# Decayed attention into a snake layer: first state in a bank of its own, 64x64 state products, diagonal states in six more blocks, and a new order

## The chip, the core and the metric

One core of a Trainium2 chip. The metric is the device time of one execution in microseconds (us). Before the change three runs gave 211.56 us in the median (211.51 to 212.55).

## What is computed

Attention with a decay `lam` per head, without softmax, over 4 batches, 8 heads, 768 positions and 64 columns, block by block with a running state, and behind it one layer of a network whose activation is h + sin(alpha h)^2 / alpha. All inputs are float32.

```python
for b in range(nb):
    intra = einsum(einsum(qb, kb) * Dmask, vb)
    inter = (qb * lam_pow) @ kv_state
    out[:, :, sl] = intra + inter
    kv_state = lam_block * kv_state + (kb * rev_pow).T @ vb
x = out as (3072 tokens, 512)
h = x @ w_in                       # 512 -> 2048
g = h + sin(alpha * h) ** 2 / alpha
result = g @ w_out                 # 2048 -> 512
```

## The kernel before

**Attention.** The kernel works with blocks of 128 positions, six to a batch, 24 in all (numbers s = 0 to 23; n = s % 6 is the place in the batch). The decay is folded into q and k when they are scaled (scale_block, L454), so that the state is a plain sum. For each block there are four kinds of work:

- S, the scores (part_S, L601): PE multiplies k by q for 8 heads into two PSUM banks, and DVE multiplies the result by a mask into the tile Sm (L623).
- O, the output (part_O, L678): PE adds v times Sm (L716) and the state times q, and ACT or DVE copies the sum from its bank into xT (L726), the input of the layer.
- Z, the state (part_Z, L637): PE adds k times v into bank 7 (ZB = 7, L1061). The bank keeps the running sum through a batch; after each block the state so far is copied out for the next block's O.
- transposes of q and k, on PE for blocks below 12 (piece_Q, piece_K, piece_T) and by DMA (L501) from block 12 on.

A state can be copied out in two forms. `diag(s)` (L630) chooses: the diagonal form goes in two halves (L666) into the tile Zd, [128, 4, 128], in which two heads stand on the diagonal of a 128x128 square and zeros beside them; O then needs four full products (`inter`, L692, matmul at L694), which `run` (L574) issues ahead of everything else in the group. The compact form is one copy (L672) into Zc, and O then needs eight products on 64x64 corners of the array (L707), behind the scores. With SD = 12 the blocks 0 to 5 and 12 to 23 are diagonal, and 6 to 11 compact.

The products of Z differ as well. Blocks 0 to 5 take four products of 128 columns, two heads by two heads, of which only the diagonal squares are used (L648; blocks 0 to 3, whose q, k and v lie two positions to a partition, take them twice with 64 rows each). Blocks from 6 on take eight products of 64 columns, one for each head (L656).

Blocks 0 to 3 are worked at the start, before the layer, from L1073 on: scores (piece_S, L790), states (piece_Z, L793), v times Sm for two blocks at once (piece_P, L746, matmul at L759), then the state's part (piece_I, L772, matmul at L779), and the copies into xT (evict, L734, copy at L739). State 0 goes into bank 7, is copied, state 1 is added in the same bank, is copied, and so on. From block 4 on, piece_G (L800) joins S of one block with O and Z of the block before.

**The layer.** Tokens go in six chunks of 512. unit_A (L807, matmul at L822) and unit_A2 (L845, matmul at L856; two output rows of half a chunk) make one or two of 16 rows of h in a bank; ACT takes the sine (L832, L866), ACT or POOL its square (L836, L837, L870, L871), and DVE adds it to h in the bank, into gT (L839, L874), which frees the bank. unit_B (L880, matmul at L887) multiplies gT by w_out for the first two chunks. The other four use seven products in place of eight (unit_P, L955, matmul at L975) with sums of the weights (weight_sums, L914, at L930) and of the tokens (token_sums, L933, at L953).

**Loads.** SP issues the loads of q, k and v. The first quarter of w_in goes through ws (load_w1_first, L373) and is cast by DVE (L384). The rest of w_in (w1, three loads, L366) and w_out (w2, four loads, L387) is cast on the way by DMAs that POOL issues. The load of q for blocks 4 and 5 waits for the second w1 load (L1100).

**Order.** Each operation is entered with what it reads and writes (_Plan.op, L114), and gets a number. `_Plan.ORDER` (L36) is a list for each engine that says in which order it takes these numbers, and by standing in a list also which of two engines takes an operation that either could. Pairs such as (8,128) in PE's list are warm-up products without use (spin, L1131). `emit` (L170) puts in the waits; `_ordered` (L163) says which dependences on the same engine need none: on PE all of them.

Of the kernel before, what the change touches and what calls it, by code (L numbers as in the profile page):

```python
# [13 lines left out]
class _Op:  # L14


    def __init__(self, eng, emit, dur, reads, writes, dma, after, issue, lat, runs=64):
# [6 lines left out]
        self.port = False  # L24
        self.after = after
# [8 lines left out]
class _Plan:  # L34
# [17 lines left out]
        ),  # L52
        "ACT": (
# [155 lines left out]
def bass_lightning_attn__then__act_snake_kernel(  # L209
# [10 lines left out]
    B, H, S, D = q.shape  # L220
# [4 lines left out]
    NB = S // BL  # L225
# [8 lines left out]
    R2 = 6  # L234
    RT = 6
    TD = 12
    SD = 12
    NP = 4
    RW = 1
    RG = 2  # L240
# [1005 lines left out]
```

## Time and profile before

| what | us |
|---|---|
| median of three runs | 211.56 (211.51 to 212.55) |
| the profiled execution | 211.5 |
| its span, first to last instruction | 209.8 |
| PE busy | 203.5 (97%) |
| DVE, ACT, POOL busy | 160.3, 158.7, 126.9 |
| last matmul's last reader (DVE, L997) starts | 207.21 |

The span is what the trace shows; the execution's own time has 1.7 us more around it. Matmuls are shown with their way through the array, so that one shown behind another begins before the first one's end. Times in the timeline are from the start of the span; "x8" merges eight instructions of one line; "[0.56 <-DVE gT L839]" is idle time ahead of the instruction, and who ended it. PEld is the loading of weights into the array. Lines such as L315 or L501 are helpers for many loads; the tile's name tells which one it is.

### The profile page before, as it was taken

The numbers are of one execution on the slowest core, as the hardware profiler recorded it, in microseconds if no ns is written. First come the engines' busy times: TensorE is split into PE (matmuls) and PEld (weight loads), VectorE is DVE, ScalarE is ACT, GpSimd is POOL, SyncE is SP. The second block draws the span as 40 slices with busy tenths as digits, with TensorE's granted clock in tenths as the row PEclk, the third lists the DMA queues.
The fourth block names the chain that finished last, engine by engine and source line by source line (L and its number), as shares of the span: only waits on it lengthen the run. The fifth ranks groups of instructions, "written<-read, shape, count | busy, mean of one in ns | idle before, by whom it ended". The sixth has DMA issues, their size and how long they took to land.

```text
span 209.8 us, 4867 instructions
## 1 busy us (share of the span) xinstructions
PE 203.5 (97%) x1975; PEld 134.3 (64%) x1975; DVE 160.3 (76%) x266; ACT 158.7 (76%) x294; POOL 126.9 (60%) x130
## 2 busy tenths in 40 slices
PE   7979999999999999999998999999999999999995
PEld 6847444457677776555555667766667765666894
DVE  4884557563999866868899799889698699777643
ACT  4949995968998989999997887787963889568210
POOL 7075354994469578679885392944581957378300
DMA  4999999999998999999999920190000004000514
GB/s 141 310 318 232 206 213 237 246 229 256 220 264 205 227 245 230 223 233 196 246 271 228 213 53 0 33 271 2 3 0 3 0 23 179 3 0 0 200 40 163
DMA packets 78998, 33.35 MB, mean 159 GB/s; under 512 B 55408, under 2 KB 76160, under 8 KB 78976
## 3 DMA queue, kind: packets, MB, share of 16 engines
q1 hardware_dynamic: 73744, 27.14, 56.2%
q0 software_dynamic: 3696, 3.67, 10.5%
q10 hardware_dynamic: 1536, 2.24, 3.3%
q8 instruction: 15, 0.25, 0.5%
q14 instruction: 7, 0.06, 0.1%
HBM read 27.28 MB, written 6.29 MB: 160 GB/s over the span
## 4 chain that ended last, share of the span: by engine, by line
PE 83%; DVE 6%; DMA 3%; SPq 3%; ACT 2%; issue 1%
PE bank L822 27%; PE bank L975 22%; PE bank L887 13%; PE bank L856 10%; DMA v<-in_v_dram 3%; PE bank L716 3%; SPq L315 3%; PE bank L612 3%; DVE gT L839 2%; PE bank L694 1%; DVE Sm L623 1%; PE bank L511 1%; PE bank L656 1%; DVE w L930 1%; PE bank L534 1%; PE bank L707 1%
## 5 line engine op out<-in xcount | busy, mean ns | idle before, releaser
L822 PE MATMUL bank<-xT,w 128*128 128x512 bf16 x296 | 70.5, 379 | 0.0
L839 DVE SCALAR_TENSOR_TENSOR gT<-u,rinv,bank 128x512 bf16<-128x512 bf16 x74 | 53.6, 742 | 18.2 <-ACT u L836 12.5
L832 ACT ACTIVATE t<-bank,alpha 128x512 bf16<-128x512 f32 x74 | 50.0, 684 | 21.0 <-PE bank L822 20.5
L822 PEld LDWEIGHTS bank<-xT,w 128*128 128x128 bf16 x296 | 28.3, 98 | 28.4 <-DVE gT L839 0.4
L836 ACT ACTIVATE u<-t 128x512 bf16<-128x512 bf16 x59 | 36.5, 628 | 1.3
L837 POOL TENSOR_TENSOR u<-t 128x512 bf16<-128x512 bf16 x15 | 16.0, 1066 | 34.1 <-ACT t L832 30.5
L953 POOL TENSOR_TENSOR gT<-gT 128x512 bf16<-128x512 bf16 x24 | 27.8, 1172 | 11.2 <-DVE Xs L953 6.0
L623 DVE TENSOR_TENSOR Sm<-bank,mask 128x1024 bf16<-128x1024 f32 x24 | 29.1, 1218 | 4.3 <-PE bank L648 1.8
L887 PE MATMUL bank<-w,gT 128*128 128x512 bf16 x128 | 31.4, 380 | 0.0
L874 DVE SCALAR_TENSOR_TENSOR gT<-u,rinv,bank 128x256 bf16<-128x256 bf16 x44 | 18.8, 476 | 7.8 <-ACT u L870 6.1
L472 POOL TENSOR_TENSOR qk<-q,Lq 128x512 bf16<-128x512 f32 x20 | 21.2, 1075 | 2.8 <-DMA q<-in_q_dram 2.8
L856 PE MATMUL bank<-xT,w 128*128 128x256 bf16 x176 | 22.2, 273 | 0.0
L492 POOL TENSOR_TENSOR qk<-k,Lk 128x512 bf16<-128x512 f32 x20 | 20.9, 1053 | 0.6 <-DMA k<-in_k_dram 0.6
L866 ACT ACTIVATE t<-bank,alpha 128x256 bf16<-128x256 f32 x44 | 18.9, 476 | 2.0 <-PE bank L856 1.5
L887 PEld LDWEIGHTS bank<-w,gT 128*128 128x128 bf16 x128 | 11.7, 98 | 12.2
L856 PEld LDWEIGHTS bank<-xT,w 128*128 128x128 bf16 x176 | 16.4, 98 | 3.5 <-issue 0.3
L953 POOL TENSOR_TENSOR Xs<-gT 128x512 bf16<-128x512 bf16 x13 | 16.1, 1235 | 1.5 <-DVE gT L839 1.4
L975 PE MATMUL bank<-w,gT 128*128 128x256 bf16 (+1 forms) x136 | 16.3, 266 | 0.0
L975 PE MATMUL bank<-w,Xs 128*128 128x256 bf16 (+1 forms) x136 | 16.0, 267 | 0.1
L975 PE MATMUL bank<-ws,gT 128*128 128x256 bf16 x128 | 15.8, 273 | 0.0
L975 PEld LDWEIGHTS bank<-w,gT 128*128 128x128 bf16 x136 | 12.6, 98 | 3.2
L975 PEld LDWEIGHTS bank<-w,Xs 128*128 128x128 bf16 x136 | 12.4, 98 | 2.8 <-DVE osb L1021 0.3
(101 smaller groups left out, 276.0 us busy)
## 6 DMA issues: line engine op xcount, KB each, us to landing
q<-in_q_dram SPq DMA_DIRECT2D x12, 512.0 KB, 6.2
k<-in_k_dram SPq DMA_DIRECT2D x24, 256.0 KB, 5.5
v<-in_v_dram SPq DMA_DIRECT2D x24, 256.0 KB, 5.4
out_dram<-osb SPq DMA_DIRECT2D x14, 256.0 KB, 2.5
w<-in_moe_w_out_dram POOLq DMA_DIRECT2D x4, 512.0 KB, 11.4
w<-in_moe_w_in_dram POOLq DMA_DIRECT2D x3, 512.0 KB, 9.0
ws<-in_moe_w_in_dram SPq DMA_DIRECT2D x2, 512.0 KB, 7.5
out_dram<-osb ACTq DMA_DIRECT2D x8, 128.0 KB, 4.0
```

The costliest lines, as they stand in the source:

```text
L472: lambda e, a=a: e.tensor_tensor(qk2[:, j:j + 2, 4 * a:4 * a + 4, :], q32[:, jq, 4 * a:4 * a + 4, :, :].rearrange("p h t d -> p t h d"), b ...
L492: lambda e: e.tensor_tensor(qk2[:, j, H:2 * H, :], block32(k32, jl), lk, ALU.mult), 1.05,
L623: op("DVE", lambda e: e.tensor_tensor(Sm[js][:, :, :], banks[:, 512 * b0:512 * b0 + 1024].rearrange("p (c i) -> p c i", i=128), bass.AP(ma ...
L822: ins = e.matmul(ps[hb][:, c0:c1], w1[:, kc, 128 * m:128 * (m + 1)], xT[x][:, kc, c0:c1], start=(kc == 0 and c0 == lo), stop=(kc == NKC - ...
L832: op("ACT", lambda e: e.activation(t16[ju][:, w], ps[hb][:, w], ACTF.Sin, scale=alpha[:, m:m + 1]), 0.69 if hi - lo == TCH else 0.475, [ba ...
L836: lambda e: (e.activation(u16[ju][:, w], t16[ju][:, w], ACTF.Square) if e is nc.scalar else e.tensor_tensor(u16[ju][:, w], t16[ju][:, w], ...
L839: op("DVE", lambda e: e.scalar_tensor_tensor(out=gT[g][:, m, w], in0=u16[ju][:, w], scalar=rinv[:, m:m + 1], in1=ps[hb][:, w], op0=ALU.mul ...
L856: ins = e.matmul(ps[hb][:, 256 * i:256 * i + 256], w1[:, kc, 128 * (m + i):128 * (m + i + 1)], xT[x][:, kc, lo:lo + 256], start=(kc == 0 a ...
L866: op("ACT", lambda e, i=i: e.activation(t16[ju][:, 256 * i:256 * i + 256], ps[hb][:, 256 * i:256 * i + 256], ACTF.Sin, scale=alpha[:, m + ...
L887: ins = e.matmul(ps[ob][:, w], gT[g][:, m, 128 * s4:128 * (s4 + 1)], w2[:, m, w], start=(m == 0), stop=(m == NM - 1),)
L953: e.tensor_tensor(dst, in0, in1, alu), 0, rd, wr))
L975: ins = e.matmul(ps[ob][:, lo + d0:lo + d1], lhs, rhs[:, d0:d1], start=first and p == 0, stop=(p == NM // 2 - 1), skip_group_check=True)
```

## The change

Four things are done.

1. **SD = 6**: all blocks are diagonal. The states of blocks 6 to 10 are copied in two halves into Zd, and blocks 7 to 11 take four full products for them in place of eight small ones. (Blocks 5, 11, 17 and 23 end a batch and have no state.)
2. **64x64 products**: the states of blocks 0 to 4 are made as those of the later blocks, eight products of 64 columns, one for each head (for blocks 0 to 3 sixteen, on 64x64 corners), and lie side by side in the first 256 columns of the bank.
3. **The first state** is summed in bank 0 and copied from there. It is summed once more in bank 7, where state 1 is added to it. This last sum waits by a semaphore for PE's own earlier sum (`drained`), as blocks 0 and 1 use different rows of the array for the same places in the bank. The scores of block 3 come before the states.
4. **The order**: new lists for all five engines, 1,046 operations in place of 1,040 (one more sum on PE, five more copies). xT of blocks 1 and 2 may now be copied by DVE or ACT. The loads of k and v for blocks 4 and 5 wait for the first w1 load.

In the new lists (numbers of before in brackets where they differ): at the start PE has

```
... 61, (8,128), 62, (3,512), 65, 69, 67, 70, (3,512), 73 [S of block 2], (2,512), 75 [S of 3], (6,512),
80 [state 0 in bank 7], 77 [state 0 in bank 0], 83 [state 1], 81 [v times Sm, 0 and 1], 86 [inter of 1],
88 [state 2], 91 [v times Sm, 2 and 3], 92, 94 [inter of 2, 3], 125, 131 [first units], ...
```

Before, state 0 (75) came ahead of S of block 3 (78), and two warm-up products stood between the inter of block 1 and state 2. POOL's list has the first w1 load ahead of the second half of v's cast (47, 103, 48, 104, 52 where it was 47, 48, 102, 103, 52), and the third w1 load (105) behind the squarings of the first unit and of the row m = 3 (128, 143), where it came ahead of all squarings. It scales k of block 5 behind q of blocks 4 and 5 and k of block 4, where it came first. SP's list has the load of k for block 5 behind q and k of block 4, where it came right behind the loads of ws. ACT takes block 0's xT copy behind the two copies of state 1; DVE takes one half of state 0 and the xT of blocks 1 and 2. PE's list has the rows m = 12 to 15 of the first chunk behind four unit_B groups, where there were six, and puts the group of block 17's scores (630, before 624) behind one more unit_P (649, before 643).

```diff
-        if d.eng != o.eng or d.dma is not None:
+        if d.eng != o.eng or d.dma is not None or o.drained:
             return False
...
-    SD = 12
+    SD = 6
...
-            def load_kv(s, which="kv"):
+            def load_kv(s, which="kv", after=()):
...
-            def part_Z(s, joined=True):
+            def part_Z(s, joined=True, zb=7, kept_state=True):
...
-                        if s < NB:
-                            for jp in range(4):
-                                ins = e.matmul(
-                                    ps[ZB][:, 128 * jp:128 * jp + 128],
-                                    qk2[r, jj, H + 2 * jp:H + 2 * jp + 2, :], v2[r, jj, 2 * jp:2 * jp + 2, :],
-                                    start=(n == 0 and jp == 0 and not t), stop=(jp == 3 and t != 0), skip_group_check=True,
-                                )
-                            continue
                         for i in range(8):
                             jp, h = i // 2, i % 2
                             ins = e.matmul(
-                                ps[ZB][64 * h:64 * h + 64, 64 * jp:64 * jp + 64],
+                                ps[zb][64 * h:64 * h + 64, 64 * jp:64 * jp + 64],
                                 qk2[r, jj, H + i, :], v2[r, jj, i, :],
-                                start=(n == 0 and jp == 0), stop=(jp == 3), skip_group_check=True,
+                                start=(n == 0 and jp == 0 and not t), stop=(jp == 3 and t != 0), skip_group_check=True,
                             )
...
-            piece_Z(0)
             piece_S(3, 5, 6)
+            first_state = run(part_Z(0, False, 0), lead_then=0)
+            run(part_Z(0, False, kept_state=False), lead_then=0)
             piece_P(0, 3, 4)
-            piece_Z(1)
+            run(part_Z(1, False), lead_then=0, drained=True)
...
-            load_kv(4)
-            load_kv(5)
+            for s in (4, 5):
+                load_kv(s, after=[last["w1", 1]])
```

More of the change, by code (lines that the diff above doesn't have):

```diff
@@ L572, in piece_K, with run @@
                        0.6, [bank(tbs[t])], [("kT", jt + t)])
-            def run(*parts, after=(), lead_then=-20):
+            def run(*parts, after=(), lead_then=-20, drained=False):
                 parts = [p for p in parts if p is not None]
@@ L586, in mm @@
                     return ins
-                op("PE", mm, 0.1 + sum(p[1] for p in parts), [b for p in parts for b in p[2]],
-                   sorted({b for p in parts for b in p[3]}), after=after)
+                o = op("PE", mm, 0.1 + sum(p[1] for p in parts), [b for p in parts for b in p[2]],
+                       sorted({b for p in parts for b in p[3]}), after=after)
+                o.drained = drained
                 lead, P.lead = P.lead, lead_then
@@ L593, in run @@
                 P.lead = lead
+                return o
             def queries(s):
@@ L663, in then @@
                 def then():
+                    if not kept_state:
+                        return
                     for h in range(2) if diag(s) else ():
                         r = slice(64 * h, 64 * h + 64)
-                        op("ACT" if s < NP else (("ACT", 0.36, 0.0), ("DVE", 0.43, 0.0)), lambda e, r=r: (e.copy if e is nc.scalar else e.tensor_copy)(
-                            Zd[s % 2][r, :, r], ps[ZB][r, :].rearrange("p (a b) -> p a b", b=128)[:, :, r] if s < NB else
-                            ps[ZB][r, 0:256].rearrange("p (a b) -> p a b", b=D)),
-                           0.36, [bank(ZB)], [("Zd", s % 2, h)])
+                        op((("ACT", 0.36, 0.0), ("DVE", 0.43, 0.0)), lambda e, r=r: (e.copy if e is nc.scalar else e.tensor_copy)(
+                            Zd[s % 2][r, :, r], ps[zb][r, 0:256].rearrange("p (a b) -> p a b", b=D)),
+                           0.36, [bank(zb)], [("Zd", s % 2, h)])
                     if diag(s):
@@ L672, in then @@
                     op((("ACT", 0.375, 0.0), ("DVE", 0.43, 0.0)), lambda e: (e.copy if e is nc.scalar else e.tensor_copy)(
-                        Zc[s % 2][:, :, :], ps[ZB][:, 0:256].rearrange("p (a b) -> p a b", b=D)),
-                       0.4, [bank(ZB)], [("Zc", s % 2)])
-                return mm, 0.37 if s < NP else 0.13 if joined else 0.25, [(w,) + y for w in ("k2", "v2") for y in of_block(s)], [bank(ZB)], then
+                        Zc[s % 2][:, :, :], ps[zb][:, 0:256].rearrange("p (a b) -> p a b", b=D)),
+                       0.4, [bank(zb)], [("Zc", s % 2)])
+                return mm, 0.18 if s < NP else 0.13 if joined else 0.25, [(w,) + y for w in ("k2", "v2") for y in of_block(s)], [bank(zb)], then
             def part_O(s, ob, ob2=None):
@@ L737, in evict @@
                 P.lead = -20
-                for eng, a0, a1, dur in (("ACT", 0, 2, 0.46), ("DVE", 2, 4, 0.4)) if len(obs) > 1 else (("ACT", 0, 4, 0.74),):
+                both = (("ACT", 0.74, 0.0), ("DVE", 0.74, 0.2))
+                for eng, a0, a1, dur in (("ACT", 0, 2, 0.46), ("DVE", 2, 4, 0.4)) if len(obs) > 1 else ((both, 0, 4, 0.74),):
                     op(eng, lambda e, a0=a0, a1=a1: (e.copy if e is nc.scalar else e.tensor_copy)(
```

5 lines of the change are left out of this document (3 added, 2 removed), and 112 rows, old and new, of the table ORDER.

## The prediction

> **What bounds the kernel now.** Read the page first (span, engines, the shares of the chain), then the table by stage, in which PE's busy time is the second number.
>
> ```profile
> span 209.8 us, 4867 instructions
> ...
> PE 203.5 (97%) x1975; PEld 134.3 (64%) x1975; DVE 160.3 (76%) x266; ACT 158.7 (76%) x294; POOL 126.9 (60%) x130
> ```
>
> ```profile
> 19.16:45.00 25.84, 25.84 (x156) 12.85 (x156) 16.19 (x25) 21.01 (x38) 15.20 (x14) 1.00 1.18 223
> 45.00:85.00 40.00, 40.00 (x472) 27.89 (x470) 30.38 (x56) 35.67 (x76) 27.69 (x27) 1.00 1.01 236
> ...
> 104.70:124.40 19.70, 19.03 (x156) 11.73 (x155) 17.83 (x24) 17.04 (x30) 13.55 (x12) 1.00 0.99 206
> 124.40:193.00 68.60, 68.60 (x570) 45.40 (x569) 58.16 (x92) 50.63 (x85) 41.37 (x38) 1.00 0.13 40
> ```
>
> From 19.16 on PE has no hole but one of 0.67 us between 104.70 and 124.40, and its granted clock is 1.00 throughout. So three things alone can move the time: when PE's long stream begins, how much work is in it, and new or vanished waits. DVE and ACT are full only where the hole lies (17.83 and 17.04 of 19.70); elsewhere an operation more on them is hidden.
>
> The beginning is seen in the chain of waits:
>
> ```profile
> 7.63 6.83 DMA v<-in_v_dram
> 14.49 0.62 ACT v L486
> ...
> 17.29 0.62 PE bank L648 x8
> ```
>
> A state is multiplied on PE (L648), copied on ACT (L666, two halves), and only then may the next state be added in the same bank. Three such rounds stand before the first unit.
>
> The rows of the start (matmul rows of PE, then the other engines):
>
> ```profile
> 14.29 0.62 PE L648 MATMUL bank<-v,qk 64*128 64x128 bf16 x8 [0.90 <-POOL v L486]
> ...
> 15.82 0.62 PE L648 MATMUL bank<-v,qk 64*128 64x128 bf16 x8
> ...
> 18.41 0.74 PE L779 MATMUL bank<-qkT,Zd 128*128 128x128 bf16 x8
> ```
>
> ```profile
> 14.17 1.70 POOL L315 DMA_DIRECT2D w<-in_moe_w_in_dram  x2
> ...
> 15.01 0.75 ACT L666 CAST Zd<-bank 64x256 bf16<-64x256 f32 x2
> ...
> 15.30 1.23 DVE L623 TENSOR_TENSOR Sm<-bank,mask 128x1024 bf16<-128x1024 f32 x1 [0.54 <-PE bank L612]
> ...
> 15.79 0.73 ACT L739 CAST xT<-bank 128x512 bf16<-128x512 f32 x1
> ...
> 16.89 0.79 DVE L384 CAST w<-ws 128x1024 bf16<-128x1024 f32 x1 [0.36 <-DMA ws<-in_moe_w_in_dram]
> ...
> 18.99 2.07 PE L856 MATMUL bank<-xT,w 128*128 128x256 bf16 x16
> ...
> 20.90 2.32 PE L822 MATMUL bank<-xT,w 128*128 128x512 bf16 x10
> ```
>
> **Part 1, diagonal states in blocks 6 to 11.** PE's stream around one block, before with the eight small products (L707), and a later block that already has the four wide ones (L694):
>
> ```profile
> 70.21 0.38 PE L887 MATMUL bank<-w,gT 128*128 128x512 bf16 x1
> 70.52 0.40 PE L612 MATMUL bank<-qkT 64*128 64x128 bf16 x8
> 70.85 0.41 PE L707 MATMUL bank<-qkT,Zc 64*64 64x128 bf16 x8
> ...
> 71.66 1.92 PE L856 MATMUL bank<-xT,w 128*128 128x256 bf16 x16
> ```
>
> ```profile
> 97.23 1.03 PE L887 MATMUL bank<-w,gT 128*128 128x512 bf16 x4
> 98.09 0.39 PE L694 MATMUL bank<-qkT,Zd 128*128 128x128 bf16 x4
> ...
> 98.98 0.29 PE L656 MATMUL bank<-v,qk 128*64 128x64 bf16 x8
> 99.21 1.04 PE L822 MATMUL bank<-xT,w 128*128 128x512 bf16 x4
> ```
>
> Count from start to start, since a duration runs past the next start (97.23 + 1.03 is 0.17 behind 98.09). One L887 product takes (98.09 - 97.23) / 4 = 0.215. The narrow block runs from 70.21 + 0.215 = 70.43 to 71.66: 1.23. The wide one from 98.09 to 99.21: 1.12. Blocks 7 to 11 read the states of 6 to 10, so five blocks gain 0.11 each: **-0.55**. What it adds: a state is copied in two halves (0.38 each on ACT, by the 15.01 row) instead of in one piece, five copies more. Between 45 and 85 ACT is busy 35.67 and DVE 30.38 of 40, so PE's stream hides them; if the cover went, the second half would hold the next block by 0.38, five times, 1.9.
>
> **Part 2, products of 64 columns in blocks 0 to 4.** Block 3, and block 4:
>
> ```profile
> 23.71 1.67 PE L822 MATMUL bank<-xT,w 128*128 128x512 bf16 x7
> 25.31 0.62 PE L648 MATMUL bank<-v,qk 64*128 64x128 bf16 x8
> 25.86 1.47 PE L822 MATMUL bank<-xT,w 128*128 128x512 bf16 x6
> ```
>
> ```profile
> 43.70 1.03 PE L887 MATMUL bank<-w,gT 128*128 128x512 bf16 x4
> ...
> 45.80 1.89 PE L887 MATMUL bank<-w,gT 128*128 128x512 bf16 x8
> ```
>
> Block 4 now takes 45.80 - 44.56 = 1.24; with the products of L656 it becomes the 1.12 of above: **-0.1**. Block 3 stops the stream from 23.71 + 7 x 0.215 = 25.22 to 25.86, 0.64. Its eight products become sixteen on 64x64 tiles, a form that no row shows for 64 columns. The nearest is L656: eight in 0.23 (98.98 to 99.21), of which some 0.1 is the change of tile shape (70.43 to 70.52), so 0.016 each; sixteen with two changes of shape: 0.45, **-0.2**. The other end is that a product costs what L648's do, (0.64 - 0.2) / 8 = 0.055, however few its columns: 1.08, +0.45. I take the first, for L656 has the same columns and the same two column groups.
>
> The Trainium skill's page "TensorEngine Tiling (Array Packing)", section "Performance Considerations", states some 60 cycles of overhead for each matmul on trn2 and advises against taking a tiling factor from a dimension that is already small: by it sixteen products of 64 columns would cost more than eight of 128. The L656 row speaks against that for the spacing of a packed stream; for the new shape no run here shows it. This is rival C below.
>
> **Part 3, the start.** The first state is summed twice, in bank 0 for the copies and in bank 7 for the running sum, so that state 1 need not wait for the copies of state 0. But in POOL's list the issue of the first w1 load now stands ahead of the second half of v's cast; both wait for the same v load, and an issue holds POOL 1.70 / 2 = 0.85. So the cast ends 0.85 later and the first state's products can begin at 15.1 instead of 14.29. PE is not idle until then: the scores of block 3 come forward (13.7), then six warm-up products of 0.215, to 15.2. From there: copy of state 0 into bank 7, state 0 in bank 0, state 1, each 16 x 0.016 = 0.26; state 1 ends at 15.2 + 0.78 + 0.17 = 16.15 (now 15.82 + 0.62 = 16.44). Its added wait is for PE's own first sum; the bank 0 sum (0.26) covers the 0.17 that this takes to land, and without it 0.17 would be lost. Behind it on PE wait all later products. ACT copies state 1 by 17.05, then block 0's xT by 17.8 and state 2 by 18.55; state 2's products begin at 17.1 (now 17.29). DVE has its half of state 0 behind the last mask (15.30 + 1.23, now some 0.5 earlier), the weight cast to 17.68, then block 1's xT, 0.73, by 18.4. The last inter products (half of the eight from 18.41 to 18.99, 0.29) follow at 18.55, and the first unit at 18.85 (now 18.99). The second needs blocks 2 and 3, which DVE and ACT have by 19.6, and starts straight behind the first at 19.72 (now there is a gap: 16 products from 18.99 to 20.90 are 1.91, of which 0.87 x 2 is work). So L822 begins at 20.6 instead of 20.90. Bounds: -0.5, if the waits go fully, to +0.85, if the late cast passes through; I take **-0.25**, the worked value less a wake-up.
>
> **Part 4, the new order.** All five lists change. The one hole first:
>
> ```profile
> 112.32 0.40 PE L694 MATMUL bank<-qkT,Zd 128*128 128x128 bf16 x4 [0.56 <-DVE gT L839]
> ```
>
> This block's output bank is freed by a gT of DVE. In the new PE list one more unit product (eight L975, some 0.87) stands ahead of this block, and on DVE the weight sum (L930) that now comes just ahead of that gT comes behind it. The wait can vanish: -0.56; a rearranged list of 1,046 operations can as well bring a few small ones. I take **-0.25**, and keep -0.6 and +1.0 for the range.
>
> Loads: k of block 5 no longer goes out behind the ws loads but behind q, gated by w1 loads.
>
> ```profile
> 24.14 0.37 SPq L315 DMA_DIRECT2D q<-in_q_dram  x1
> ```
>
> q waits for the second w1 load already now (24.14), and the first lands before the second on one queue, so the new wait of k and v costs SP nothing; what is behind it was behind q. That frees one 256 KB transfer ahead of the weights. In return POOL scales k of block 5 only behind q and k of block 4:
>
> ```profile
> 38.24 1.05 POOL L492 TENSOR_TENSOR qk<-k,Lk 128x512 bf16<-128x512 f32 x1
> ...
> 42.18 0.39 PE L511 MATMUL bank<-ident,qk 128*128 128x128 bf16 x4
> ```
>
> That is 38.24 + 2 x 1.05 = 40.3, and its transposes, now at 42.18, come at some 41: still hidden.
>
> **Sum.** -0.55 - 0.1 - 0.2 - 0.25 - 0.25 = -1.35, from the profiled execution's 211.5 (its span is 209.8; the median of the runs is 211.56, the same): **210.1**.
>
> **Rivals.** **B, the order gives it back.** PE saves 0.85 in parts 1 and 2, but the start gains nothing and new waits of 0.3 to 1.0 appear where DVE and ACT are full (17.83 of 19.70). For it: lists packed for one kernel's timing have margins of tenths. Against: the table shows a single hole now. 211.5 - 0.85 + 0.3 = 210.95 to 211.7; say 211.1.
>
> **C, narrow products are no cheaper.** Block 3 then costs +0.45, and the three sums at the start 0.88 each instead of 0.26: 1.86 more, of which the earlier readiness takes up 0.25. 211.5 - 0.65 + 0.45 + 1.6 - 0.25 = 212.65.
>
> **D, slower: the last w1 load comes late.** Its issue moves on POOL behind two squarings (L837, L871), which wait for the first units.
>
> ```profile
> 17.97 0.75 POOL L315 DMA_DIRECT2D w<-in_moe_w_in_dram  x1
> ...
> 22.96 1.04 POOL L837 TENSOR_TENSOR u<-t 128x512 bf16<-128x512 bf16 x1 [4.24 <-ACT t L832]
> ```
>
> ```profile
> 33.69 0.81 POOL L315 DMA_DIRECT2D w<-in_moe_w_out_dram  x1 [2.85 <-DMA w<-in_moe_w_in_dram]
> ...
> 35.37 3.62 PE L822 MATMUL bank<-xT,w 128*128 128x512 bf16 x16
> ```
>
> It goes out at some 23.5 instead of 17.97, it lands now at 33.65 (the 33.69 row waits for it), and the columns that it brings are used from 35.37, in the new list two L887 groups (0.86 each) sooner and 0.45 sooner by parts 2 and 3: from 33.2. If two loads are still under way ahead of it at 23.5 (it takes 15.7 from issue to landing now, so it stands in a queue), nothing changes and the absent k brings it forward by one transfer, some 1.0, to 32.7. If it lands 5.5 later like its issue, at 39.2, PE stands still for 6.0: 216.1. It decides from 33.2 on; from 34.5 on the whole gain is gone, from 35.6 on the kernel is slower by over 0.5%.
>
> The Trainium skill's page "DMA: Bandwidth & Descriptors", section "Queues, rings and completion order", says that each DMA engine takes turns between the queues that have work, packet by packet. By that POOL's queue keeps its share as long as it isn't empty, which speaks for the first case; how many packets wait there no view shows.
>
> **Chances.** Forecast 0.62 (209.3 to 210.5), B 0.22, C 0.04, D 0.09, rest 0.03. About 0.5% is what a measurement of this kernel can tell from no change: below 210.5 is faster, above 212.6 slower. Faster: 0.58 of the forecast and 0.03 of B, 0.61. Slower: C half, D, 0.11. Same: 0.28. The range leaves out D and half of C and the rest: 209.2 to 211.8.
>
> **What would show it.** Right: L694 four times in blocks 7 to 11 and 1.12 from start to start; block 3's interruption 0.45; the first L856 at 18.85 and L822 at 20.6; no wait at the block near 111. Wrong: sixteen products in over 0.6 (C); a wait of PE on the w1 load near 33 (D); PE holes with DVE or ACT as releaser between 85 and 125 (B); v's second cast followed by an idle PE near 15 and the first unit after 19.

## The result, and the profile after

| | before | after |
|---|---|---|
| median of four runs | 212.06 us (211.51 to 213.56) | 218.86 us (217.34 to 220.28) |
| the profiled execution | 211.5 | 219.11 |
| its span | 209.8 | 217.3 |

The ratio is 1.036, 95% interval 1.030 to 1.042: slower by 3.6%, where 210.1 us was forecast. Some kernels below have their times in two groups; a ratio given here is that of the lower group, with the disturbed runs left out.

The kernel after has its own line numbers: L819 was L822 (unit_A's product), L853 was L856 (unit_A2), L836 was L839 (gT), L884 was L887 (unit_B), L927 was L930 (weight sums), L690 was L694 and L776 was L779 (diagonal states times q), L651 was L656 (state products of 64 columns), L663 was L666 (state copies), L615 was L612 (scores), L972 was L975 (unit_P), L473 and L493 were L472 and L492 (scaling of q and k on POOL), L1132 was L1134 (warm-up products).

First the page: engines' busy time, then the granted clock in 40 slices of 5.4 us.

```profile
span 217.3 us, 4968 instructions
...
PE 207.5 (96%) x2017; PEld 136.6 (63%) x2017; DVE 167.0 (77%) x273; ACT 156.5 (72%) x292; POOL 125.2 (58%) x130
...
PEclk9999999759999999999999999999999999999999
```

PE is busy for 4.0 us more than before and idle for 3.5 us more (217.3 - 207.5 against 209.8 - 203.5), and in the eighth and ninth slice the clock is down. Most of both lies in one place. The waits of PE (total, times, longest):

```profile
PE bank L819 <- DVE gT L836: 4.0, 3, 3.6
```

One wait of 3.6 us on a gT of DVE; the longest wait on another engine was 1.5 before, at the very start. The table by stretch around it (length, then PE, PEld, DVE, ACT, POOL busy, granted clock, DMA share, GB/s):

```profile
38.40:42.20 3.80, 0.20 (x1) 0.00 (x1) 3.80 (x3) 1.68 (x4) 2.53 (x3) 0.84 1.05 177
42.20:44.00 1.80, 1.80 (x5) 0.70 (x6) 1.26 (x2) 0.00 (x0) 0.00 (x0) 0.50 1.11 237
44.00:46.00 2.00, 2.00 (x9) 0.90 (x8) 0.00 (x0) 1.84 (x3) 1.98 (x1) 0.50 0.73 162
46.00:48.00 2.00, 2.00 (x12) 1.05 (x10) 1.31 (x3) 0.00 (x1) 2.00 (x2) 0.55 0.72 172
48.00:50.00 2.00, 2.00 (x13) 0.89 (x11) 1.02 (x3) 0.72 (x2) 2.00 (x3) 1.00 1.09 309
```

PE does nothing for 3.6 us, then runs with half its clock until 48: a loss of 3.8 x 0.5 + 2.0 x 0.45 = 2.8. The first products behind the wait:

```profile
42.20 1.89 PE L819 MATMUL bank<-xT,w 128*128 128x512 bf16 x4 [3.61 <-DVE gT L836]
```

What DVE did instead of the gT, and what POOL did then:

```profile
35.56 0.75 DVE L836 SCALAR_TENSOR_TENSOR gT<-u,rinv,bank 128x512 bf16<-128x512 bf16 x1 [0.52 <-ACT u L833]
36.22 5.27 DVE L927 TENSOR_TENSOR Ta<-w 128x1024 bf16<-128x1024 bf16 x1
41.41 2.05 DVE L836 SCALAR_TENSOR_TENSOR gT<-u,rinv,bank 128x512 bf16<-128x512 bf16 x3
```

```profile
36.07 0.81 POOL L316 DMA_DIRECT2D w<-in_moe_w_out_dram  x1
36.89 2.05 POOL L473 TENSOR_TENSOR qk<-q,Lq 128x512 bf16<-128x512 f32 x2
38.90 2.03 POOL L493 TENSOR_TENSOR qk<-k,Lk 128x512 bf16<-128x512 f32 x2
44.02 2.12 POOL L927 TENSOR_TENSOR ws<-w 128x1024 bf16<-128x1024 bf16 x1 [3.08 <-DMA w<-in_moe_w_out_dram]
```

The weight sum Ta takes 5.27 us. It begins 0.15 behind POOL's issue of a w_out load and ends 0.56 behind the last of four scalings that follow without a pause (38.90 + 2.03 = 40.93), which is about the sum's own length when nothing disturbs it. That length is in the trace of before, where POOL at that time stands idle (its 33.69 row names 2.85 us of idle time ahead of it):

```profile
32.86 0.68 DVE L930 TENSOR_TENSOR Ta<-w 128x1024 bf16<-128x1024 bf16 x1
```

The second place is the start. PE's rows:

```profile
1.52 4.10 PE L1132 MATMUL bank<-Xs 128*128 128x112 bf16 x42 [1.52 <-DVE Xs L411]
```

```profile
14.60 0.42 PE L615 MATMUL bank<-qkT 64*64 64x128 bf16 x16
14.95 1.47 PE L1132 MATMUL bank<-Xs 128*128 128x512 bf16 x6
16.35 0.84 PE L651 MATMUL bank<-v,qk 64*64 64x64 bf16 x42
...
20.62 0.22 PE L776 MATMUL bank<-qkT,Zd 128*128 128x128 bf16 x1 [0.72 <-issue]
20.67 0.60 PE L853 MATMUL bank<-xT,w 128*128 128x256 bf16 x4
```

The first unit begins at 20.67 (before 18.99, forecast 18.85). Ahead of it one single product stands behind 0.72 us for which the profile names no releaser ("issue").

The parts that the forecast named, in the later stream: block 3, block 4, a block with the newly diagonal state, and the block of the old wait near 111.

```profile
22.42 1.89 PE L819 MATMUL bank<-xT,w 128*128 128x512 bf16 x8
24.24 0.44 PE L651 MATMUL bank<-v,qk 64*64 64x64 bf16 x16
24.61 3.63 PE L819 MATMUL bank<-xT,w 128*128 128x512 bf16 x16
```

```profile
52.33 0.39 PE L690 MATMUL bank<-qkT,Zd 128*128 128x128 bf16 x4
...
53.44 1.90 PE L884 MATMUL bank<-w,gT 128*128 128x512 bf16 x8
```

```profile
78.20 0.39 PE L690 MATMUL bank<-qkT,Zd 128*128 128x128 bf16 x4
...
79.31 1.92 PE L853 MATMUL bank<-xT,w 128*128 128x256 bf16 x16
```

```profile
115.56 1.89 PE L819 MATMUL bank<-xT,w 128*128 128x512 bf16 x8 [0.18 <-DVE gT L836]
```

Added up by what stands where: the first unit is 1.68 late; block 3's interruption is 0.18 shorter; block 4 is 0.13 shorter; the hole adds 3.61 and the clock 2.8. That makes 7.8; the L884 products behind block 4 begin at 53.44, 7.64 later than before (45.80). From there to the last reader (214.38, before 207.21) the difference shrinks to 7.17: five blocks save 0.11 each and the wait near 111 saves 0.38, while new gaps of 0.27 and 0.42 take most of that back (some 0.2 is not assigned).

### The profile page after: what moved, and what is told of

Its sections match the earlier page's. It is cut to its first block, busy times and chain, and to the rows that moved or that the text cites. A ratio compares the mean times of both kernels' runs of the same rounds, so it can differ in the third digit from the quotient of the medians.

```text
span 217.3 us, 4968 instructions
## 1 busy us (share of the span) xinstructions
PE 207.5 (96%) x2017; PEld 136.6 (63%) x2017; DVE 167.0 (77%) x273; ACT 156.5 (72%) x292; POOL 125.2 (58%) x130
## 4 chain that ended last, share of the span: by engine, by line
PE 85%; DVE 8%; ACT 4%; issue 1%; ACTq 0%
PE bank L819 27%; PE bank L972 23%; PE bank L884 10%; PE bank L853 9%; PE bank L1132 5%; PE bank L615 3%; DVE gT L836 3%; DVE Ta L927 2%; PE bank L712 2%; PE bank L535 2%; PE bank L690 1%; PE bank L651 1%; ACT Zd L663 1%; PE bank L512 1%; DVE gT L950 1%
## 5 line engine op out<-in xcount | busy, mean ns | idle before, releaser
L819 PE MATMUL bank<-xT,w 128*128 128x512 bf16 x296 | 71.9, 383 | 4.0 <-DVE gT L836 4.0
L836 DVE SCALAR_TENSOR_TENSOR gT<-u,rinv,bank 128x512 bf16<-128x512 bf16 x74 | 53.9, 743 | 19.1 <-ACT u L833 13.5
L819 PEld LDWEIGHTS bank<-xT,w 128*128 128x128 bf16 x296 | 28.0, 98 | 32.9 <-DVE gT L836 5.1
L833 ACT ACTIVATE u<-t 128x512 bf16<-128x512 bf16 x61 | 37.9, 629 | 1.2
L950 POOL TENSOR_TENSOR gT<-gT 128x512 bf16<-128x512 bf16 x22 | 26.1, 1192 | 14.4 <-PE bank L972 5.8
L884 PE MATMUL bank<-w,gT 128*128 128x512 bf16 x128 | 33.2, 394 | 0.0
L834 POOL TENSOR_TENSOR u<-t 128x512 bf16<-128x512 bf16 x13 | 13.4, 1040 | 22.0 <-ACT t L829 22.0
L473 POOL TENSOR_TENSOR qk<-q,Lq 128x512 bf16<-128x512 f32 x20 | 21.5, 1088 | 2.6 <-DMA q<-in_q_dram 2.6
L853 PE MATMUL bank<-xT,w 128*128 128x256 bf16 x176 | 22.2, 273 | 0.0
L493 POOL TENSOR_TENSOR qk<-k,Lk 128x512 bf16<-128x512 f32 x20 | 21.3, 1073 | 0.0
L884 PEld LDWEIGHTS bank<-w,gT 128*128 128x128 bf16 x128 | 12.2, 101 | 13.4 <-issue 1.9
L868 POOL TENSOR_TENSOR u<-t 128x512 bf16<-128x512 bf16 x8 | 8.3, 1040 | 19.2 <-ACT t L863 17.1
L853 PEld LDWEIGHTS bank<-xT,w 128*128 128x128 bf16 x176 | 16.4, 98 | 3.8 <-DVE xT L736 0.8
L972 PE MATMUL bank<-w,gT 128*128 128x256 bf16 (+1 forms) x136 | 16.1, 266 | 0.0
L972 PE MATMUL bank<-w,Xs 128*128 128x256 bf16 (+1 forms) x136 | 15.8, 266 | 0.0
L972 PE MATMUL bank<-ws,gT 128*128 128x256 bf16 x128 | 15.8, 273 | 0.0
L972 PEld LDWEIGHTS bank<-w,gT 128*128 128x128 bf16 x136 | 12.8, 98 | 3.5
```

What stands on the lines that cost most here:

```text
L473: lambda e, a=a: e.tensor_tensor(qk2[:, j:j + 2, 4 * a:4 * a + 4, :], q32[:, jq, 4 * a:4 * a + 4, :, :].rearrange("p h t d -> p t h d"), b ...
L493: lambda e: e.tensor_tensor(qk2[:, j, H:2 * H, :], block32(k32, jl), lk, ALU.mult), 1.05,
L819: ins = e.matmul(ps[hb][:, c0:c1], w1[:, kc, 128 * m:128 * (m + 1)], xT[x][:, kc, c0:c1], start=(kc == 0 and c0 == lo), stop=(kc == NKC - ...
L833: lambda e: (e.activation(u16[ju][:, w], t16[ju][:, w], ACTF.Square) if e is nc.scalar else e.tensor_tensor(u16[ju][:, w], t16[ju][:, w], ...
L836: op("DVE", lambda e: e.scalar_tensor_tensor(out=gT[g][:, m, w], in0=u16[ju][:, w], scalar=rinv[:, m:m + 1], in1=ps[hb][:, w], op0=ALU.mul ...
L853: ins = e.matmul(ps[hb][:, 256 * i:256 * i + 256], w1[:, kc, 128 * (m + i):128 * (m + i + 1)], xT[x][:, kc, lo:lo + 256], start=(kc == 0 a ...
```

## The experiments

The theory on the hole: DVE's sum and POOL's work exclude each other, and the new order puts the sum where POOL starts a long unbroken run, so that it ends 4.6 us late, the gT behind it waits, PE stands, and the standing costs the clock as well. The rivals: that something else in the new order would hold that gT back without the sum too; and, on the mechanism, that the run alone does it, or that it takes the issue. In the expectations theory 1 and its later forms 1a and 1b are about this lock, theory 2 about the start, and theory F about a hole of PE at the start. Ratios are to the kernel before on the same chip.

### The sum taken off DVE

```diff
 DVE: ..., 435, 179,
-436,
 175, 187, ...
 POOL: ..., 198, 200,
+436,
 437, 439, ...
```

> The changed kernel with one operation moved: the weight sum that stood 5.27 us on DVE at 36.22 (first half of Ta, L927) goes to POOL, ahead of POOL's sum that waited for a load from 40.94 to 44.02. Theory 1 (DVE's sum is locked out by POOL's unbroken run of operations, PE then stands 3.6 us and its clock falls): no wait of PE over 0.3 us between 30 and 56, granted clock 1.00 from there on, and 218.86 - 6.4 = 212.5 us. Rival 1 (the late gT comes from late loads or from the new order of gT, the long DVE row is only where it shows): the hole of PE stays at 38 to 42 or moves by under 1 us, 217 to 219. Theory 2 (the start alone costs 1.7 us whatever happens at 36): first unit product (L853) again at 20.3 to 20.9.

212.73 us, ratio 1.010 (1.007 to 1.012). The table of the same stretch:

```profile
38.00:42.00 4.00, 3.95 (x26) 2.01 (x25) 2.98 (x5) 3.46 (x7) 4.00 (x4) 1.00 1.13 205
```

One of 1,046 operations on another engine, and the hole and the half clock are both gone: by the ratios (1.036 - 1.010) x 211 = 5.5 us, by the medians 6.1. The kernel is still 1% slower than before. In the profiled execution (span 211.1, 1.3 more than before) the first unit is 1.34 late:

```profile
15.53 0.84 PE L651 MATMUL bank<-v,qk 64*64 64x64 bf16 x42
...
20.28 0.22 PE L776 MATMUL bank<-qkT,Zd 128*128 128x128 bf16 x1 [1.21 <-issue]
20.33 0.93 PE L853 MATMUL bank<-xT,w 128*128 128x256 bf16 x7
```

### The same sum put beside POOL's work in the old order

```diff
 DVE (before): ..., 162, 166,
-430,
 178, 174, 429, 186,
+430,
 190, 208, ...
```

> The kernel before with the same sum moved later on DVE, from 32.86 to behind the gT at 37.82, so that it starts inside POOL's run of 36.24 to 43.53. Theory 1: the sum then lasts until POOL's run ends, 4 to 5.5 us instead of 0.68, the gT behind it are late by as much, PE stands 2.5 to 4 us near 40 to 44 and its granted clock falls to 0.5 for some us: 216 to 219 us. Rival 1 (a sum of 0.7 us later in the list costs 0.7 at most): 211.5 to 212.8, clock 1.00.

210.86 us, ratio 1.001 (0.9996 to 1.002): nothing.

```profile
38.44 1.51 DVE L930 TENSOR_TENSOR Ta<-w 128x1024 bf16<-128x1024 bf16 x1
```

The sum is held, but only until POOL's next operation would begin; then DVE gets its turn. So in its first form, "DVE waits for the end of POOL's run", the theory was wrong. Next the sum beside four scalings in a row (430 behind 216):

> The kernel before with the Ta sum of DVE moved behind the first mask of block 4 (42.94), so that it starts near 44.2, inside four scalings in a row on POOL (q, q, k, k from 43.87 to 47.94). Theory 1a, formed after e2, where the sum of DVE got in between a scaling and a weight sum of POOL at 39.36: POOL keeps the port from one operation to the next of the same form, and DVE gets in only where the form changes or POOL pauses. Then the row lasts 3.5 to 4.5 us and the mask of block 5 behind it (46.0) comes 2 us late; PE stands 1 to 2.5 us near 47, 212.5 to 215. Rival 1a (DVE gets in at the next boundary of any two operations, and the 5.27 us of the changed kernel came from the DMA issue ahead of the run): at most 1.7 us, no wait of PE, 210.8 as before.

211.28 us, ratio 1.001 (0.999 to 1.003).

```profile
44.11 1.36 DVE L930 TENSOR_TENSOR Ta<-w 128x1024 bf16<-128x1024 bf16 x1
```

```profile
43.88 2.49 POOL L472 TENSOR_TENSOR qk<-q,Lq 128x512 bf16<-128x512 f32 x2
46.34 2.04 POOL L492 TENSOR_TENSOR qk<-k,Lk 128x512 bf16<-128x512 f32 x2
```

Again let in at the first boundary; POOL's first two scalings take 2.49 instead of 2.04, so from the boundary on it is POOL that waits. An unbroken run of scalings is not enough. What the new order has besides is the issue.

### The run broken, and the issue moved

In the changed kernel, first one of POOL's own sums put between the scalings of q and of k, then the issue put behind those of q:

```diff
 POOL (e8): ..., 108, 170,
-434,
 174, 109, 196, 197,
+434,
 198, 200, ...
```

```diff
 POOL (e9): ..., 170, 434, 174,
-109,
 196, 197,
+109,
 198, 200, ...
```

> The changed kernel with one operation of POOL moved: the weight sum of 31.9 (2.1 us) goes between the q and the k scalings of blocks 4 and 5, so that the run of four of one form becomes two, a sum, two. DVE's sum stays where it is (36.22). Theory 1a: it gets in where the form changes, at 38.9, and lasts 3.3 us instead of 5.27; PE stands 1.5 to 2.2 us instead of 3.61, and the granted clock falls for less long or not at all: 213.5 to 217. Rival 1 (POOL must pause for DVE to get in): the row lasts until 43.5, 7 us or more, and PE stands over 5 us: over 220. Rival 1b (DVE gets in at any boundary once the DMA issue is over): the row lasts 1.4 us, under 213.

220.88 us, ratio 1.046 (1.042 to 1.050): worse than the changed kernel.

```profile
36.46 7.33 DVE L927 TENSOR_TENSOR Ta<-w 128x1024 bf16<-128x1024 bf16 x1
```

The sum begins 0.15 into the issue (36.31), and is held through five operations of POOL to its pause, 7.33. A sum between the scalings does not break the hold.

> The changed kernel with POOL's last DMA issue (w_out, 36.07) moved behind the two q scalings; DVE's sum stays in its place, on DVE, and POOL's run stays unbroken. Theory 1b, after e5 and e8 (in e5 DVE got in at the next boundary of a run without an issue, in e8 it did not through a whole run that began with one): a sum that starts inside a DMA issue is locked out until POOL pauses, one that starts inside a scaling only until that scaling ends. Then the sum, which now starts with a scaling, lasts 1.3 to 1.7 us, PE has no wait over 0.5 us near 40, and the time is 212.3 to 213.5, as e1. Rival 1 (any run without a pause locks it out): 4 to 5.5 us as in the changed kernel, 217 to 220.

```profile
36.14 1.45 DVE L927 TENSOR_TENSOR Ta<-w 128x1024 bf16<-128x1024 bf16 x1
```

Same sum, same place on DVE, same four scalings, no issue under way when it begins: 1.45 instead of 5.27. Its time does not show this: one run took 213.38 us, as forecast, but three took 216.68 to 217.19. In the profiled one (216.74) the later issue lets PE wait on the load itself:

```profile
PE bank L884 <- DMA w<-in_moe_w_out_dram: 2.3, 1, 2.3
```

The counter-test was to bring the issue under the sum in the kernel before (DVE's 430 behind 186, POOL's issue 108 behind 196):

> The kernel e2 (before, Ta sum of DVE behind the gT of 37.8) with POOL's last w_out issue moved from 33.7 to behind the two q scalings, 38.3 to 39.1, so that DVE's sum starts at 38.44 inside it. Theory 1b: the sum lasts until POOL pauses (one scaling and at least one weight sum later, 42.2 or later): 3.8 us or more, against 1.51 in e2; PE stands 1 to 4 us, 213 to 219. Rival (the issue is no worse than another operation): the sum lasts 1.3 to 1.7 us and the time stays at 210.9 to 211.5; a wait of PE on the later w_out load itself would show as a DMA releaser.

It missed its aim: the sum began 0.22 ahead of the issue (38.54 and 38.76), not in it, and took 0.83. The time, 216.95 us (ratio 1.027, 1.023 to 1.032), comes from another wait, again on the later load:

```profile
PE bank L887 <- DMA w<-in_moe_w_out_dram: 4.0, 1, 4.0
```

### The clock

The changed kernel with fourteen warm-up products of 512 columns ahead of the held unit product. They add constants to an open output bank, so that one block of the output is not the reference's.

```diff
 PE: ..., 192, 232,
+(14, 512),
 188, 234, ...
```

> The changed kernel with 14 products of 512 columns (3.0 us) more on PE ahead of the unit that waits for DVE's late gT at 42.2; they add constants to an output bank, so one output block isn't the reference's. Theory of the clock (the granted clock falls to 0.5 because PE stood still): the hole is filled, the unit begins at 42.2 as before, the clock stays 1.00 behind it and the time is 218.86 - 2.8 = 216.1. Rival (the clock falls for another reason, or its fall costs nothing): 218 to 219.5, or more by up to 3 if the products themselves come in the way.

215.73 us, ratio 1.021 (1.019 to 1.024). The hole is filled with useless work, and the work behind it runs at the full clock:

```profile
41.92 1.04 PE L819 MATMUL bank<-xT,w 128*128 128x512 bf16 x4 [0.59 <-DVE gT L836]
```

```profile
42.20:44.00 1.80, 1.80 (x15) 0.97 (x14) 0.98 (x2) 0.97 (x2) 0.09 (x1) 1.00 1.25 264
```

Four unit products take 1.04, not 1.89. The gT comes no sooner: the unit begins 41.92 - 35.79 = 6.13 behind POOL's issue, and 42.20 - 36.07 = 6.13 in the changed kernel. So 218.86 - 215.73 = 3.1 us is the price of the clock, by itself.

### The start

On top of e1, four kernels change PE's lists. In e4 the first two groups of warm-up products become few and long; in e6 four groups further on do, and e7 takes out besides the six of 512 columns ahead of the first state, and lets DVE copy its half of state 0 earlier.

```diff
 PE (e4)
-(42,112), 39, (30,128), 57
+(10,470), 39, (8,480), 57
```

```diff
 PE (e6)
-(7,128), 55, (5,128), 53, 59, (6,128), 61, (8,128)
+(2,448), 55, (2,320), 53, 59, (2,384), 61, (2,512)
 PE (e7, besides)
-(2,512), 75, (6,512), 80
+(2,512), 75, 80
 DVE (e7)
-74, 76, 79
+74, 79, 76
```

> As e1, and the first 72 warm-up products of PE (42 of 112 columns, 30 of 128) replaced by 18 of 470 and 480 columns, which take as long: 54 products, or 108 instructions with their weight loads, fewer ahead of the first unit. Theory F (the hole of 0.94 us from start to start inside the last inter group at 19.68, ended by nothing that the profile shows, is PE out of instructions, because many short products use up the fetched block): the hole is gone from that group, first unit at 19.7 to 20.0, some 0.7 us less than e1. Rival (the hole has another cause, such as a landing load): it stays at the same product, first unit as in e1, time as e1 within 0.3 us.

212.14 us, ratio 1.004 (1.001 to 1.007). The hole is no longer in the last inter group but earlier, among the products of v and Sm for blocks 0 and 1:

```profile
18.64 0.41 PE L756 MATMUL bank<-Sm,v 64*64 64x128 bf16 x14 [0.91 <-issue]
```

Count PE's products and weight loads up to the hole, by the table of stretches (x behind PE and PEld). Some traces, that of e4 among them (1,937 products for 1,963 weight loads), lack some records of products, so take two in which none is missing: the changed kernel, and e13 (below), where such a hole stands after as many weight loads, 222, as in e4:

```profile
0.00:20.60 20.60, 17.98 (x348) 14.19 (x349) 14.56 (x26) 11.82 (x25) 9.76 (x24) 1.00 1.00 249
```

```profile
0.00:17.30 17.30, 14.12 (x221) 11.15 (x222) 12.29 (x23) 9.73 (x20) 9.73 (x24) 1.00 0.95 256
...
17.45 0.33 PE L651 MATMUL bank<-v,qk 64*64 64x64 bf16 x7 [1.69 <-issue]
```

That is 697 and 443. The traces hold eight and six more instructions of PE up to there (semaphores and one drain, which the tables do not count): 705 and 449, 256 apart. The hole sits at one of two counts of instructions, not at a dependence.

> As e1, and 26 warm-up products of 128 columns between the transposes of the start replaced by 8 of 320 to 512 columns, as long in all: 18 products or 36 instructions fewer ahead of the first unit. Theory F (PE out of fetched instructions after 703 to 705 products and weight loads in e1 and in the changed kernel, after 447 in e4, 256 apart): 36 fewer shift the end of the block to 17 products behind the first unit's start, by when the next block has come; no hole in the inter groups, first unit at 19.0 to 19.3 instead of 20.33, time 1.0 to 1.3 us under e1, 211.5. Rival (hole of another cause): the hole stays at the fourth product of the last inter group, time within 0.3 us of e1.

212.4 us (eight of eleven runs, 211.54 to 214.08; the other three 217.61 to 219.08), ratio 1.007 (1.004 to 1.010). With 18 products and as many weight loads fewer ahead of the units than in e1 the hole has moved into the second unit, behind 348 weight loads (349 in e1):

```profile
22.18 1.68 PE L819 MATMUL bank<-xT,w 128*128 128x512 bf16 x7 [0.79 <-issue]
```

> As e6, without the six warm-up products of 512 columns (1.4 us) that stand between the scores of block 3 and the first state, and with DVE's half of state 0 ahead of the mask of block 3. Theory 2 (those six hold the chain of states): first state's products at 14.2 to 14.9 instead of 15.5, first unit at 17.9 to 18.6, 0.5 to 1.0 us under e6. Rival (the copies, not the products, set the rounds; or the v casts and the loads do): first unit within 0.3 of e6.

210.1 us (eight of ten runs, 209.80 to 212.41; the other two 213.0 and 214.3), ratio 0.998 (0.995 to 1.001); no such hole in its profile, and the first unit is ahead of the old kernel's 18.99:

```profile
14.23 0.93 PE L651 MATMUL bank<-v,qk 64*64 64x64 bf16 x43
...
18.31 1.98 PE L853 MATMUL bank<-xT,w 128*128 128x256 bf16 x16 [0.37 <-DVE xT L736]
```

So the six products were in the way of the first state by about their own length: from the start of block 3's scores to the first state it is 14.23 - 13.95 = 0.28 here and 16.06 - 14.31 = 1.75 in e6. Of these 1.47 the first unit gets 0.8 (from the same scores 4.36 here, 5.17 in e6); waits on the copies of ACT and DVE take the rest.

### Parts 1 and 2 alone, in the old order

SD = 6 and the 64x64 products in the kernel before, its lists kept; the one copy of each new diagonal state becomes two at the same place.

```diff
-    SD = 12
+    SD = 6
...
-                        if s < NB:
...
-                            continue
```

> The kernel before with only the diagonal states of blocks 6 to 10 and the 64x64 products, in the old order (each compact copy becomes two halves at the same place of the same list), no second sum of the first state. Steps 1 and 2 of the prediction: 0.85 us less, 211.2 against 212.06 (the block around L694 1.12 from start to start, block 3 interrupted for 0.45). Rival C (64-column products cost what those of 128 do): 0.45 more at block 3 and 0.9 to 1.2 more at the start, 212.8 to 213.2. Rival B (the second halves of the copies come late): new waits of PE on ACT or DVE at blocks 7 to 11 of 0.38 each, up to 213.

211.03 us, ratio 1.001 (0.999 to 1.003): the 0.85 that the blocks save did not arrive. Its profiled execution (212.21, the slowest of them, with a granted clock of 0.57 from 16 to 20) shows where it went. Set beside the kernel before, unit by unit, e3 is 0.96 us late behind the first unit and 0.68 late behind block 4 (first weight load of the next unit at 46.48 against 45.80): the 0.3 of part 2 is there. But a unit behind block 11 loads its first weights at 81.25, where before it did at 79.84, 1.41 late. The stretch of blocks 7 to 11 has lost 0.73, where part 1 forecast a gain of 0.55. The wide blocks do take 1.12; beside them stand small waits that the kernel before does not have, such as this (L847 is L856 of before, L865 the gT of L874):

```profile
60.50 2.18 PE L847 MATMUL bank<-xT,w 128*128 128x256 bf16 x16
62.52 0.39 PE L511 MATMUL bank<-ident,qk 128*128 128x128 bf16 x4
```

```profile
61.64 0.77 PEld L847 LDWEIGHTS bank<-xT,w 128*128 128x128 bf16 x8 [0.38 <-DVE gT L865]
```

Sixteen products that take 1.75 before (59.71 to 61.46) are 2.02 from start to start, as the second eight wait for a gT of DVE. That is what rival B of this run's expectation says in kind; which of the added copies makes DVE late was not isolated.

### A version that is faster, and two tests on it

e7 with the next weight sum on DVE (438) two places later, behind 252:

> As e7, and the last weight sum that DVE still has near 43 (ws, second half, which in one profile of e6 lasted 6.30 us) moved behind the copy of 49.7, where POOL pauses. Theory 1: the runs of e7 between 211.5 and 214.3 were such lock-outs, so no run lies over 211 and the median is 209.8 to 210.0, ratio to before 0.995. Rival (they have another cause): runs over 211 stay as frequent as in e7, four in ten.

209.69 us (209.58 to 210.48), ratio 0.993 (0.991 to 0.995): faster than before by 0.7%. None of six runs is over 210.5, where in e7 four of ten were over 211.5, as theory 1 said, though six runs are few. The first unit begins at 18.39, and no wait of PE on DVE is over 0.4. Here the parts arrive: the last reader starts at 205.29, 1.92 ahead of before. Of this 0.60 is the start and 1.32 the stream behind it, for which parts 1 and 2 (0.85) and the old hole (0.56) together promise 1.41. In this kernel the sum 436 went back to DVE:

> The kernel e11 with the Ta sum back on DVE, in its place in the changed list, where it would now start near 34.0, inside POOL's w_out issue (33.85 to 34.65), with two q scalings straight behind it and a short pause at 36.7. Theory 1b (a sum that starts inside an issue stays locked out over the boundaries of the run until POOL pauses): 2.7 to 3.4 us, the gT behind it 2.5 us late, PE stands 1 to 2.5 us near 36, 211 to 214. Rival (the issue is as any other operation; what decides is something else): 1.2 to 1.4 us, no wait of PE over 0.5 us, 209.7 as e11.

Of twelve runs six took 209.83 to 211.93 us (ratio 0.998, 0.996 to 1.001) and six 215.47 to 220.27. The profiled execution, 219.41, is one of the latter. PE stands 1.69 us at its start (the row in the section on the start), so the sum comes not near 34.0 but at 37.02, 0.16 into an issue at 36.86, and is held again. No profile shows what the sum does in the six shorter runs:

```profile
37.02 5.26 DVE L927 TENSOR_TENSOR Ta<-w 128x1024 bf16<-128x1024 bf16 x1
```

In e14 the first state is summed once, in bank 7, as before the change:

> The kernel e11 with the first state summed once, in bank 7, and copied from there; state 1 waits for its two copies again, all lists otherwise the same (one operation fewer on PE). If the bank of its own is worth what the prediction's part 3 gave to it: the first unit 0.3 to 0.8 us later than the 18.3 of e7 and e11, 210.0 to 210.5. Rival (the copies of state 1 on ACT set the rounds either way, behind the copy of state 0): first unit within 0.2 us, 209.7.

210.1 us (ten of twelve runs, 209.63 to 211.25; the other two 213.5), ratio 0.996 (0.993 to 0.998), overlapping with e11.

```profile
15.12 0.41 PE L651 MATMUL bank<-v,qk 64*64 64x64 bf16 x16
16.27 0.34 PE L651 MATMUL bank<-v,qk 64*64 64x64 bf16 x10 [0.73 <-DVE Zd L663]
...
19.17 1.91 PE L853 MATMUL bank<-xT,w 128*128 128x256 bf16 x16
```

The second state waits 0.73 for the copy of the first, as Part 3 says, but from the first state to the first unit it is 4.05 here and 18.39 - 14.26 = 4.13 in e11. The bank of its own brings nothing that these runs can show: the chain ends in DVE's and ACT's copies either way.

## Why the prediction was wrong, step by step

**What bounds the kernel: the step that failed.** It says that DVE is full only where the hole lies and that "elsewhere an operation more on them is hidden". DVE was in fact not full ahead of the hole (its 35.56 row has 0.52 us of idle time before it). But the question was not how full DVE is; it was how long one operation takes there. 0.68 us in a place where POOL is idle became 5.27 beside POOL's issue and scalings. A share of busy time says nothing of that. In the sum the step is part 4, the new order, taken at -0.25 with +1.0 at worst: it cost 3.61 of standing and 2.8 of clock, +6.4. The clock was read as 1.00 throughout and left out of the three things that can move the time. The forecast had both halves before it: it worked out that k of block 5 would be scaled behind q and k of block 4, so that POOL's run grows, and called it "still hidden", looking only at who waits for k; and it counted on the sum that moves behind a gT at 111, without looking where the other sum, Ta, goes. Taking it off DVE gives 5.5 to 6.1 us back (e1), and 3.1 of them are the clock (e12).

The Trainium skill's page "SBUF — State Buffer", section "Who interferes with whom", has the rule that would have raised the question: a DVE operation with two inputs in SBUF contends with a GpSimd operation that reads SBUF, the shared ports are an exclusive lock, and issue order decides who blocks. The runs agree for one operation (1.51 in e2, 1.36 in e5, 1.45 in e9). Held for one operation, the sum would have cost some 0.8 more (1.51 against 0.68), within the range; that DVE is held through four or five further operations (5.27, 7.33) is not in that rule, and here the measurement decides.

**Part 1** was right in its size: 79.31 - 78.20 = 1.11 for 1.12, and 1.11 and 1.12 in the two other blocks of that form (72.83, 82.28); the two without scores in the group save 0.12 each as well. **Part 2** too: block 3 is interrupted from 22.42 + 8 x 0.215 = 24.14 to 24.61, 0.47 for 0.45; block 4 takes 53.44 - 52.33 = 1.11 for 1.12. So **rival C** is out: sixteen products of 64 columns take 0.37 (24.24 to 24.61), 0.023 each, not 0.055. But the sum counted what the blocks save as saved by the kernel, and e3 shows that in the old order new waits took it back.

**Part 3.** The chain itself was worked out well: 3.65 was forecast from the first state to the first unit, and it is 20.67 - 16.35 - 0.72 = 3.60, and 20.33 - 15.53 - 1.21 = 3.59 in e1, once the hole is taken out. The cast of v was not late: it ended at 13.56 + 0.62 = 14.18, before the change at 13.61 + 0.62 = 14.23, as the issue ahead of it went out at 12.60 already. Two terms were missing, and part 3 came to +1.68 in place of -0.25. The first state began at 16.35 and not at 15.2: 0.82 of that is a slower PE at the very start of this execution (e1 has the same lists there and begins at 15.53; the first 42 warm-up products took 4.10 against 3.48 in e1, both at a granted clock of 1.00), the rest a small error of the working. And PE stood for 0.72 (1.21 in e1) at a count of its instructions, waiting for nothing that the profile shows. That six warm-up products were put ahead of the first state was seen, but taken for cover of the late cast; they were most of the wait (e7).

The Trainium skill's page "Runtime: NRT & Kernel Launch", section "Instruction fetch mechanics", says that each engine's instructions are fetched in blocks of 256, and that crossing a block is mostly hidden. The 256 between the holes' counts in the changed kernel and e13 agree; "hidden" does not, with 0.72 us (changed kernel), 1.21 (e1) and 1.69 (e13) here, behind a stretch in which PE used its instructions up quickly.

**Part 4's** hole went nearly as said (0.56 to 0.18). **Rival D** did not happen: no wait of PE on a w1 load. **Rival B** was the right kind, new waits by the order, but looked for them where the engines are full and gave them 0.3 to 1.0; the wait came from an operation that grew, at 38, and cost 6.4. Only rival D had a stop of that size (6.0), from a late load, and no rival asked what a stop does to the clock.

## What to carry to other kernels

When an order changes, look for each DVE operation with two SBUF inputs at what POOL does beside it in the new order, a DMA issue above all; its duration in the old profile holds only for the old neighbour. Price a new stop of PE with the clock that it loses behind it, which here nearly doubled it. And a saving in PE's stream is a saving only if what feeds the stream can follow: try the parts without the new order before adding them up.

## What the runs showed of the hardware that was not expected

- One DVE operation of 0.68 us was held for 5.27 (changed kernel and e12), 7.33 (e8) and 5.26 (e13) when it began 0.15 to 0.16 into a DMA issue of POOL, and for 1.36 to 1.51 beside scalings alone. What decides it stays open. In the profiled execution of e6 a sum that began 0.37 into a sum of POOL was held for 6.30, through four scalings, with no issue under way; the same sum was let in at the next boundary in e1 (1.33), e4 (1.21) and e7 (1.05). The test that would have forced it in the old kernel (e10) missed by 0.22.
- After 3.6 us without work PE's granted clock was 0.50 to 0.55 for nearly 6 us of work; 3.1 us of time. Shorter stops did it too: after 2.3 us (e9) it was 0.50 to 0.52 from 46.5 to 49.5, and after 1.69 us (e13) 0.50 to 0.54 from 17.6 to 21.0. After 1.21 us (e1) it stayed at 1.00.
- Holes of 0.7 to 1.7 us without a releaser stood 256 instructions of PE apart, and moved with the number of small products ahead of them. That fetching causes them is argued from this count, not shown by a record of the fetch, and in e7 and e11 no such hole shows.
- The first 42 warm-up products took 4.10 in one execution and 3.48 in another, at a granted clock of 1.00 in both; the start moved by 0.8 with it.
